# Value gradients of a recurrent attention's backward loop: from the memory keys alone to all 40 keys of a step

## The chip, the cores and the metric

One core of one Trainium2 chip runs the whole program. Its engines work side by side, each through its own list of instructions in a fixed order, and wait for one another by semaphores: TensorE (PE, with its weight loads PEld), VectorE (DVE), ScalarE (ACT), GpSimd (POOL) and the queue engine SyncE (SP), which only issues transfers. POOL issues transfers too, and each of those takes a place in its list. The metric is the device time of one launch in microseconds (us), the median of several runs.

## What is computed

The reference is the forward and the backward pass of one block: a layer norm, a recurrent attention A with a memory of 8 rows, a gated MLP B, and `out = x + A * silu(B)`. Outputs are `out` and the gradients of nine inputs, in bf16. The part that matters here is A's recurrence, cut from the reference:

```python
for s in range(n_seg):                     # S = 2048 rows, segments of 32: 64 steps
    xs = x[:, s * 32:(s + 1) * 32, :]
    h = concatenate([mem, xs], axis=1)     # 8 memory rows and 32 x rows
    q, k, v = (einsum('btd,dhe->bhte', h, W) for W in (Wq, Wk, Wv))   # 32 heads of 128
    p = softmax(where(mask, q @ k.T * scale, -1e9))
    o = einsum('bhqk,bhke->bhqe', p, v)
    o = einsum('bhte,hed->btd', o, Wo)
    mem = o[:, :8, :]                      # goes into the next step
    outs.append(o[:, 8:, :])
```

D is 640, so a weight is 640 x 4096. In the backward pass the steps run from the last to the first. The gradient of `v` of one step is, head by head, `p.T @ g`, where `g` is the gradient of the attention's output before `Wo`, over all 40 queries of the step. For the row gradient, `gv @ Wv.T` is added to `gk @ Wk.T` and `gq @ Wq.T`. The mask lets x queries see memory keys and earlier x keys, and memory queries see all 40 keys.

## The kernel before

The program runs in stages: layer norm and the forward pass of B; the forward recurrence of A (`recurrence`); the backward recurrence (`phase4_Abwd`, some 1810 to 2898 us of the profile); the weight stage (`phase6_Awgrads`, 2898 to about 4113 us), which forms the weight gradients of Wv, Wk and Wq and the row gradients of the x rows; the gradient of Wo; and the backward pass of B. In each stage `in_order` pins every engine to the written order.

**The backward loop.** `chain(t, gap)` is one step, t from 63 to 0. It holds a dependent chain: what it computes for the 8 memory rows is the gradient that the step before needs. Between its links it calls `gap("W0")`, `gap("W1")`, `gap("G1")` to `gap("G6")`, and `gap_of` fills each gap with work on the x rows, which depends on nothing in the chain. That work is cut into units: one tile of three steps (120 rows) and four heads (`tl, qd`). A unit goes through `ld` (transfers), `turn` (transposes of v and g rows), `dprob` (gradient of p), `dsoft` (gradient of the scores), `gmem` (what the x queries give to the memory keys, and to the memory values). Two or three units ride in each of 59 steps; the first ones are done ahead of the loop, and the last four steps have none.

The chain of a step, in the order of PE:

- `packed_half` twice (L306): the 32 rows in `gox` (8 memory rows, 24 x rows of a later step that ride along) times WoT, four column groups of 32 packed in the array; the result is copied to `sg` by DVE and by ACT, and stored to GOS by SP.
- `packed_sel` twice (L314): picks the 8 memory rows per group and turns them; DVE copies them to `gmT` (L1213).
- Two transposes of `gmT` (L1220), copied to `gOst`; 32 products of `gmT` with the turned values `vT` (`dprob_m`, L1226).
- `gkv(1, gOst, bdP)` (L1195, L1197): the value gradients of the 8 memory keys. `bdP` is the block diagonal of the memory queries' p, made by POOL at the step's start (L1182); `xp` adds what the x queries gave in `gmem`, loaded from GXP.
- `packed_out(gvT, WvT)` (L325): 64 matmuls, 8 weight columns each and 320 columns moving, into bank `pm`; 20 of them, then the transposes of the softmax gradient (L1236), then 44. DVE meanwhile forms `dS`.
- `gkv(0, ...)`, `packed_out(gkT, WkT)`, the q gradients (L1262), `packed_out(gqT, WqT)`: the same for k and q, all summed in `pm`.
- `fold_add` (L334, L336): ACT and DVE add the bank's two halves to `fs`. `fold_turn` (L352) turns it, DVE copies it to the next `gox` (L1283), and PE begins the next step. `fold_store` (L343) has POOL store the 8 memory rows, as two transfers.

`WARM = dict(G4=1)` puts one 128x512 product without use (L1430) between `fold_add` and `fold_turn`. The buffers that hold one step's loads are `vTb`, `Pm` and `Qsts` (two each of the last two), two `krbs` and one `xpb`. SP issues the loads in the written order: `loads` (L1151 to L1156), `load_k` (L1162 to L1169), `load_xp` (L1174), and `ld` for the units (L1307, L265, L1311). `ps.tile(..., tag="x", bufs=5)` are the five PSUM buffers that the units share.

**The weight stage.** Eight rounds of four heads (`qd`), 22 units each. `Fetch.ld` loads five units ahead: rows of DSR, PR and of g, q and k, with the memory rows fetched by POOL (`load_m`, L245). `s1` transposes dS, `s2` forms the row gradients of v, k and q from p or dS and the rows (i = 0, 1, 2), `s3` transposes these three for the x rows into `ring` (L1630), and `s4` multiplies them with WvT, WkT and WqT of the four heads, twelve matmuls per 128 rows and half of D, added into `acc` over the rounds (L1648, L1654). `wg` then forms the weight gradients of the round (L1667, three times 100 matmuls).

Of the kernel before, what the change touches and what calls it, by code (L numbers as in the profile page):

```python
# [16 lines left out]
P = 128  # L17
# [23 lines left out]
class K:  # L41
# [109 lines left out]
    def setup_dram(self):  # L151
# [15 lines left out]
        self.GXA = mk("GXA", (S, D))  # L167
        self.HRO = mk("HRO", (self.NR, D))
# [22 lines left out]
        self.GXP = mk("GXP", (self.NTL, P, 8, 3, 2, 32), F32)  # L191
# [6 lines left out]
        self.PM = mk("PM", (T, P, 80))  # L198
# [57 lines left out]
    def g_src(self, tl, c0, c1):  # L256
        nx = self.geo(tl)[2]
        x0 = 96 * tl
        if x0 >= self.GB0:
            return [(0, nx, self.GX0[x0 - self.GB0:x0 - self.GB0 + nx, c0:c1])]  # L260
        return [(0, 96, self.blk_src("g", 2 + tl, 0, 96, c0, c1))]

# [67 lines left out]
def fold_add(k, pm, pool, tag="fup"):  # L330

    fs = pool.tile([64, 320], BF16, name="fsum", tag="fsum")
    up = pool.tile([64, 320], F32, name="fup", tag=tag)
    k.nc.scalar.copy(up[:], pm[64:128, 0:320])  # L334
    for c in (0, 160):
        k.nc.vector.tensor_tensor(fs[:, c:c + 160], pm[0:64, c:c + 160], up[:, c:c + 160], ALU.add)  # L336
    return fs


def fold_store(eng, dst, fs):  # L340

    for b in range(2):
        eng.dma_start(dst[:, 320 * b:320 * b + 320], fs[32 * b:32 * b + 8, :])  # L343
# [211 lines left out]
def recurrence(k, W0, W4, Wv, Wk_, Wq, Wo, own, ps, banks):  # L555
    nc, tc = k.nc, k.tc
    D, DC, S, H, HD, T = k.D, k.DC, k.S, k.H, k.HD, k.T
    with tc.tile_pool(name="achain", bufs=1) as ch, \
# [39 lines left out]
        def chain(t, gap):  # L598
# [71 lines left out]
            nc.gpsimd.dma_start(k.PM[t].rearrange("p (a c) -> p a c", a=2), Pm[:])  # L670
# [24 lines left out]
            fs = fold_add(k, pm, ch)  # L695
# [387 lines left out]
def phase4_Abwd(k, out2, W0, W4, WT, own, ps, banks):  # L1083
# [20 lines left out]
    with tc.tile_pool(name="gst", bufs=1) as st, tc.tile_pool(name="gchain", bufs=1) as ch, \  # L1104
# [10 lines left out]
        Qsts = [two(k0[:, c:c + 256]) for c in (3072, 3328)]  # L1115
# [3 lines left out]
        bds = [PTs[1][:, 2 * i:2 * i + 2, :].rearrange("p a (h c) -> p a h c", c=8) for i in range(2)]  # L1119
        krbs = [st.tile([120, 2048], BF16, name="krb")[:], vt[0:120]]  # L1120
        bdm = st.tile([P, 16, 8], BF16, name="bdm")
        b16 = st.tile([P, 16], F32, name="b16")
        xpb = st.tile([P, 8, 2, 32], F32, name="xp")
# [6 lines left out]
        WARM = dict(G4=1)  # L1130
# [16 lines left out]
        def loads(t):  # L1147
# [4 lines left out]
            Pm = ch.tile([P, 2, 40], BF16, name="gPm", tag="gPm", bufs=2)  # L1152
            nc.sync.dma_start(Pm[:], k.PM[t].rearrange("p (a c) -> p a c", a=2))
            Qst = Qsts[t % 2]
            for a in range(2):
                nc.sync.dma_start(Qst[:, a, :], k.QM[t, :, a * 2048:(a + 1) * 2048])  # L1156
            ins[t] = vT, Pm, Qst

        def load_k(t):
            kr = krbs[t % 2][0:104]  # L1160
# [17 lines left out]
        def bd(eng, dst, src):  # L1178
            for a in range(2):
                v = src[:, a, 0:8]  # L1180
                v = bass.AP(tensor=v.tensor, offset=v.offset, ap=[list(v.ap[0]), [0, 16], list(v.ap[1])])
                eng.tensor_tensor(dst[:, a], bdm[:], v, ALU.mult)  # L1182

        def chain(t, gap):
# [3 lines left out]
            vT, Pm, Qst = ins.pop(t)  # L1188
            xp = xps.pop(t)
            bdP, bdS = bds  # L1190
            bd(nc.gpsimd, bdP, Pm)
            def gkv(i, lh, rh):
                pk = bB[:, 256 * i:256 * i + 256].rearrange("p (a c) -> p a c", a=2)
                for a in range(2):
                    nc.tensor.matmul(pk[:, a, :], lh[:, a, :], rh[:, a].rearrange("p h m -> p (h m)"), start=True, stop=True)  # L1195
                g_ = ch.tile([P, H, 8], BF16, name="gkv", tag=f"gkv{i}")
                nc.vector.scalar_tensor_tensor(g_[:].rearrange("p (u h) m -> p u (h m)", h=4),  # L1197
                                               pk.rearrange("p a (u c) -> p (a u) c", c=32), k.scale if i == 0 else 1.0,
                                               xp[:, :, i, :], op0=ALU.mult, op1=ALU.add)
                return g_  # L1200

            sg = ch.tile([P, 1024], BF16, name="gstg", tag="gstg", bufs=1)
# [6 lines left out]
            gap("W0")  # L1209
            packed_sel(k, pg, sg, 1)  # L1210
            gmT = ch.tile([P, 2, 8, 16], BF16, name="gmT", tag="gmT")
# [3 lines left out]
            nc.sync.dma_start(k.GOS[t // 4, :, :, t % 4].rearrange("g r c -> (g r) c"), sg[:])  # L1215
            gap("W1")
            gOst = ch.tile([P, 2, P], BF16, name="gOst", tag="gOst")
            pgo = bview(bB, P, 2, P, bf=True)
            for a in range(2):
                nc.tensor.transpose(pgo[:, a, :], gmT[:, a].rearrange("p q h -> p (q h)"), k.ident[:])  # L1220
            nc.vector.tensor_copy(gOst[:], pgo[:])
# [6 lines left out]
            gvT = gkv(1, gOst, bdP)  # L1228
            dprob_m(1)
            dPT = ch.tile([40, 2, P], BF16, name="dPT", tag="dPT")  # L1230
            nc.scalar.copy(dPT[:], psd.rearrange("p a q h -> p a (q h)"))
            gap("G1")
            packed_out(k, pm, gvT, WvT, True, False, 0, 5)
# [3 lines left out]
            pr = ch.tile([P, 2, 40], F32, name="gpr", tag="gpr")  # L1237
            nc.vector.tensor_tensor(pr[:], ps2[:], Pm[:], ALU.mult)
            Dm = ch.tile([P, 2], F32, name="Dm", tag="Dm")
            nc.vector.tensor_reduce(Dm[:], pr[:], axis=AX.X, op=ALU.add)  # L1240
            u = ch.tile([P, 2, 40], F32, name="gu", tag="gpr")
            nc.vector.tensor_tensor(u[:], ps2[:], bc_last(Dm[:], 40), ALU.subtract)
            dS = ch.tile([P, 2, 40], BF16, name="dSm", tag="dSm", bufs=2)
            nc.vector.tensor_tensor(dS[:], u[:], Pm[:], ALU.mult)
# [3 lines left out]
            packed_out(k, pm, gvT, WvT, False, False, 5, 16)  # L1248
            gkT = gkv(0, Qst, bdS)
# [3 lines left out]
            dST = ch.tile([104, 8, 16], BF16, name="dSTm", tag="dPT")  # L1253
# [10 lines left out]
            gqT = ch.tile([P, H, 8], BF16, name="gqT", tag="gqT")  # L1264
# [13 lines left out]
            fs = fold_add(k, pm, ch, "gstg")  # L1278
# [5 lines left out]
            fold_store(nc.gpsimd, k.m_rows(k.GWO, t - 1) if t > 0 else out2f, fs)  # L1284
            gap("G6")

# [71 lines left out]
        def gmem(tl, qd):  # L1358
# [4 lines left out]
            pk = ps.tile([P, 2, 4, nm], F32, name="gkp", tag="x", bufs=5)  # L1363
# [187 lines left out]
def phase6_Awgrads(k, X, W0, fetch, out0, out3, out4, out5):  # L1551
# [13 lines left out]
    with tc.tile_pool(name="h6i", bufs=3) as io, tc.tile_pool(name="h6", bufs=1) as hp, \  # L1565
# [136 lines left out]
        for _ in head(0):  # L1702
            pass
# [588 lines left out]
```

## Time and profile before

| | us |
|---|---|
| median of 3 runs (4697.81 to 4703.79) | 4698.75 |
| the profiled execution | 4684.61 |
| its span | 4682.7 |
| PE busy in the weight stage's matmuls L1648 | 459.9 |
| PE busy in its transposes L1630, gr rows | 134.5 |
| PE busy in the weight gradients L1667 | 521.7 |
| PE waiting for `fold_add` before L352 in the loop (62 times) | 24.0 |

How to read it: PE's busy time is the union of its matmuls, whose ends are modelled. So a group's busy time divided by its count gives what one costs in the stream, while "mean ns" is the length of one with its pipeline. In the lists in order of time, the first column is the start, the second the length of the whole group (x40 means forty instructions), and a bracket holds the idle time before it and what ended it. In the stage tables each pair of brackets holds an instruction count; the last three columns are the TensorE clock granted (1.00 is full speed), the mean busy share of the 16 DMA engines, and GB/s. A wait is put down to the engine whose semaphore came last.

### The profile page before, as it was taken

Reading aid. Unit: us, or ns where it says so; the run is one execution under the profiler, and the core shown is the slowest. Engines: PE = TensorE matmul, PEld = TensorE weight load, DVE = VectorE, ACT = ScalarE, POOL = GpSimd, SP = SyncE. Lnnn points to the kernel's source line nnn. Section 1 sums busy time; section 2 is a strip of 40 time slices with the busy share of each in tenths; the row PEclk is TensorE's granted clock in tenths of the full one; section 3 lists DMA queues with packets and bytes.
Section 4 is the critical chain, followed back from the end, with each engine's and each line's share of the span. In section 5 each row is a group of like instructions: output and inputs, shape, how many; then the busy total and the mean of one; then the engine's idle time right before and its main releaser. Section 6 shows DMA issues by size and latency. Waiting matters only on the chain. (4 is left out here: it accounts for less than half of the span.)

```text
span 4682.7 us, 159785 instructions
## 1 busy us (share of the span) xinstructions
PE 4466.5 (95%) x64504; PEld 2821.1 (60%) x64504; DVE 2244.7 (48%) x7156; ACT 1587.4 (34%) x4360; POOL 2098.4 (45%) x3528
## 2 busy tenths in 40 slices
PE   8999999999999898999999998999999999999999
PEld 4544555555555555666666665676667666666675
DVE  8734666666666534555555553343224432311460
ACT  5432555555544433333333332232223322200000
POOL 6532555555555423455444444354335533311440
PEclk9999999999999998999999999999999999999999
DMA  8773566666655677777777775664345543579783
GB/s 269 236 252 119 175 178 178 179 179 179 180 168 167 167 181 230 211 225 207 215 211 209 208 209 154 144 163 132 110 116 158 147 129 107 170 223 207 159 181 100
DMA packets 976843, 834.77 MB, mean 178 GB/s; under 512 B 518890, under 2 KB 858286, under 8 KB 974144
## 3 DMA queue, kind: packets, MB, share of 16 engines
q1 hardware_dynamic: 763879, 547.92, 42.2%
q0 software_dynamic: 129952, 228.13, 16.4%
q10 hardware_dynamic: 82275, 48.52, 4.0%
q8 instruction: 509, 8.34, 0.8%
q14 instruction: 228, 1.87, 0.1%
HBM read 472.66 MB, written 310.33 MB: 167 GB/s over the span
## 5 line engine op out<-in xcount | busy, mean ns | idle before, releaser
L1667 PE MATMUL wg<-gr,hr 128*128 128x512 bf16 x2400 | 521.7, 379 | 0.0
L1648 PE MATMUL g<-land,ghacc 128*128 128x320 bf16 x3072 | 459.9, 300 | 0.8
L1667 PEld LDWEIGHTS <-hr 128*128 128x128 bf16 x2400 | 233.9, 98 | 278.9
L306 PEld LDWEIGHTS <-hx 128*32 128x32 bf16 x10240 | 246.8, 96 | 229.1 <-issue 14.6
L1648 PEld LDWEIGHTS <-ghacc 128*128 128x128 bf16 x3072 | 289.2, 98 | 104.2 <-ACT ghacc L92 2.2
L90 DVE CAST wgo<-wg 128x512 bf16<-128x512 f32 x72 | 49.8, 692 | 471.2 <-PE wg L1667 471.2
L90 DVE CAST stg<-bank 128x512 bf16<-128x512 f32 x256 | 177.1, 692 | 158.6 <-PE bank L306 154.5
L880 POOL DMA_DIRECT2D OR<-xv x163 | 89.8, 551 | 361.1 <-ACT xv L92 338.5
L1613 POOL DMA_DIRECT2D GSP<-grs x48 | 25.5, 542 | 473.1 <-ACT grs L1605 472.0
L92 ACT COPY ghacc<-t6g 128x768 bf16<-128x768 bf16 (+1 forms) x176 | 137.1, 779 | 293.8 <-PE t6g L1630 284.5
L1324 POOL DMA_DIRECT2D VTD<-gvT x176 | 129.4, 742 | 218.7 <-ACT gvT L1323 209.5
L325 PEld LDWEIGHTS <-gkv 128*8 128x8 bf16 x8192 | 177.6, 86 | 82.2 <-issue 4.1
L832 POOL TENSOR_TENSOR xP<-xP,xrz 120x480 bf16<-120x480 bf16 x163 | 161.1, 988 | 76.0 <-DVE xrz L831 46.6
L812 ACT ACTIVATE xP<-xsp,xnm 120x120 bf16<-120x120 f32 (+1 forms) x540 | 186.1, 372 | 26.0 <-DVE xnm L794 25.9
L1654 DVE TENSOR_TENSOR ghacc<-ghacc,g 128x320 f32<-128x320 f32 x192 | 93.6, 487 | 209.9 <-PE g L1648 209.9
L336 DVE TENSOR_TENSOR fsum<-bank,fup 64x160 bf16<-64x160 f32 x254 | 69.5, 311 | 258.5 <-ACT fup L334 255.2
L92 ACT CAST wgo<-wg 128x512 bf16<-128x512 f32 x48 | 28.1, 585 | 479.8 <-PE wg L1667 407.0
L1371 POOL DMA_DIRECT2D GXP<-gks x157 | 91.0, 580 | 189.5 <-ACT gks L1369 188.8
L325 PE MATMUL bank<-Wo,oTm 128*32 128x320 bf16 x4032 | 154.2, 307 | 18.4 <-DVE oTm L684 18.4
L325 PE MATMUL bank<-WkT,gkv 128*8 128x320 bf16 x4096 | 162.8, 299 | 4.2 <-issue 2.2
L325 PE MATMUL bank<-WvT,gkv 128*8 128x320 bf16 x4096 | 166.4, 305 | 0.5 <-DVE gkv L1197 0.5
L306 PE MATMUL bank<-Wq,hx 128*32 128x512 bf16 x2560 | 161.6, 381 | 0.0
(389 smaller groups left out, 10916.1 us busy)
## 6 DMA issues: line engine op xcount, KB each, us to landing
QVS<-stg SPq DMA_DIRECT2D x128, 256.0 KB
kT<-VTD SPq DMA_DIRECT2D x64, 320.0 KB
PR<-xP POOLq DMA_DIRECT2D x168, 120.0 KB, 3.1
VTD<-gvT POOLq DMA_DIRECT2D x168, 120.0 KB, 4.0
land<-DSR SPq DMA_DIRECT2D x168, 120.0 KB
land<-PR SPq DMA_DIRECT2D x168, 120.0 KB
OR<-xv POOLq DMA_DIRECT2D x163, 120.0 KB, 3.0
orr<-OR SPq DMA_DIRECT2D x14, 1280.0 KB
```

What stands on the lines that cost most here:

```text
L90: return nc.vector.tensor_copy(out, in_)
L92: return nc.scalar.copy(out, in_)
L306: k.nc.tensor.matmul(bank[32 * g:32 * g + 32, :], x[:, dc, :], W[:, dc, c0:c0 + 512], start=(dc == 0), stop=(dc == k.DC - 1), tile_positio ...
L325: k.nc.tensor.matmul(pm[p0:p0 + nq, 0:320], x[:, h, :], W[:, h, 320 * b:320 * b + 320], start=(first and i == 0), stop=(last and i == 15), ...
L812: nc.scalar.activation(Pb[0:n, j, 0:n], sp[0:n, j, :], ACT.Exp, bias=nmx[0:n, j:j + 1], scale=k.scale, accum_out=Z[0:n, j:j + 1])
L832: eng.tensor_tensor(Pb[0:n, :, 0:n], Pb[0:n, :, 0:n], bc_last(rz[0:n], n), ALU.mult)
L880: q.dma_start(k.OR[120 * tl:120 * tl + n, c0:c0 + 512], v[0:n])
L1324: nc.gpsimd.dma_start(k.VTD[tl][:, :, h0:h0 + 4, :], vTq[:])
L1371: (nc.sync if (tl, qd) in pro else nc.gpsimd).dma_start(k.GXP[tl, :, qd, 0:ns], ks[:].rearrange("p s i h m -> p s i (h m)"))
L1648: nc.tensor.matmul(pg[:], ring[:, i, j, r0:r0 + P], Ws[qd][i][:, j, 320 * h:320 * h + 320], start=(i == 0 and j == 0), stop=(i == 2 and j ...
L1654: nc.vector.tensor_tensor(a, a, pg[:], ALU.add)
L1667: nc.tensor.matmul(pw[:], hr[:, tl, dc * P:(dc + 1) * P], grs[i][:, tl, :], start=(tl == 0), stop=(tl == NF - 1))
```

## The change

The value gradients of all 40 keys of a step are now formed in the chain. `vgrad` multiplies, per head, the 32 x rows of g (`xr`, loaded by SP) with their p (`prx`), and the 8 memory rows (`sg`) with theirs (`prm`): heads are split over four groups of 32 partitions, so 32 matmuls of 32 rows and 32 of 8 rows per step, 40 columns each, summed in four PSUM banks. ACT and DVE copy them to `gv`. `packed_out` takes the first 32 keys (8 of memory, 24 of x) in place of 8. The last 8 x keys of four steps are gathered in `lv` by POOL, and `extra` puts them through a packed product of their own every fourth step. The x rows' part of `gv @ Wv.T` is stored in a new tensor GXV, and the weight stage adds it once, in round 0, instead of forming it: `s3` and `s4` run over k and q alone. `gmem` and GXP lose their value half. To make room in SBUF, buffers are shared or single where they were two (`Pm`, `Qst`, `krb`, `fsum`, `seq`), and the useless product goes; the first unit's `turn` moves from W0 into the gap G4 of the step before, the second one's from W1 to G1. In the weight stage q's memory rows are loaded by SP, and the loads of `hr` are cut finer.

```diff
-def fold_add(k, pm, pool, tag="fup"):
+def fold_add(k, pm, up, fs):
...
-def fold_store(eng, dst, fs):
+def fold_store(eng, dst, fs, r0=0):
     for b in range(2):
-        eng.dma_start(dst[:, 320 * b:320 * b + 320], fs[32 * b:32 * b + 8, :])
+        eng.dma_start(dst[:, 320 * b:320 * b + 320], fs[32 * b + r0:32 * b + r0 + dst.shape[0], :])
...
-        WARM = dict(G4=1)
+        WARM = {}
...
+        def load_g(t):
+            tl, s = t // 3, t % 3
+            nc.sync.dma_start(xr, k.g_rows(t))
+            nc.sync.dma_start(prf, k.PR[tl][32 * s:32 * s + 32].rearrange("q (g h) c -> g q (h c)", g=4))
+            for g in range(4):
+                nc.sync.dma_start(prm[32 * g:32 * g + 8],
+                                  k.PM[t, g // 2].rearrange("(q b h) c -> b q h c", q=8, b=2)[g % 2])
+
+        def prx_copy(t):
+            tl, s = t // 3, t % 3
+            nx = k.geo(tl)[2]
+            nc.gpsimd.tensor_copy(prx[:, :, 8:40], prf[:, :, 32 * s:32 * s + 32])
+            nc.gpsimd.tensor_copy(prx[:, :, 0:8], prf[:, :, nx + 8 * s:nx + 8 * s + 8])
+
+        def vgrad(vb, lh, rh, n, j0, j1, first):
+            for j in range(j0, j1):
+                for g in range(4):
+                    p0 = 32 * g
+                    nc.tensor.matmul(vb[g][:, j, :], lh[p0:p0 + n, j * P:(j + 1) * P], rh[p0:p0 + n, j, :],
+                                     start=first and j == 0, stop=not first and j == 7, tile_position=(p0, 0), skip_group_check=True)
+
+        def extra(m, bank):
+            packed_out(k, bank, lv, WvT, True, True)
+            fs = fold_add(k, bank, up, ch.tile([64, 320], BF16, name="fsum", tag="fsum"))
+            for b in range(2):
+                nc.gpsimd.dma_start(k.GXV[128 * m:128 * m + 128, 320 * b:320 * b + 320].rearrange("(t r) d -> t r d", r=32)[:, 24:32],
+                                    fs[32 * b:32 * b + 32, :])
...
-            kr = krbs[t % 2][0:104]
+            kr = krbs[1][0:104]
...
-            bd(nc.gpsimd, bdP, Pm)
...
             packed_sel(k, pg, sg, 0)
             gap("W0")
+            vb = [bview(b_, P, 8, 40) for b_ in [bA] + [ps.tile([P, 512], F32, name="gvx", tag="x", bufs=5) for _ in range(3)]]
+            vgrad(vb, xr, prx, 32, 0, 8, True)
+            vgrad(vb, sg, prm, 8, 0, 4, False)
             packed_sel(k, pg, sg, 1)
...
+            vgrad(vb, sg, prm, 8, 4, 8, False)
...
+            if t > 0:
+                load_g(t - 1)
+            for g, e in ((0, 's'), (2, 'v'), (1, 's'), (3, 'v')):
+                k.copy(gv[:, 8 * g:8 * g + 8, :], vb[g], eng=e)
+            nc.gpsimd.tensor_copy(lv[:, :, 8 * (t % 4):8 * (t % 4) + 8], gv[:, :, 32:40])
             gap("W1")
-            gOst = ch.tile([P, 2, P], BF16, name="gOst", tag="gOst")
-            pgo = bview(bB, P, 2, P, bf=True)
-            for a in range(2):
-                nc.tensor.transpose(pgo[:, a, :], gmT[:, a].rearrange("p q h -> p (q h)"), k.ident[:])
-            nc.vector.tensor_copy(gOst[:], pgo[:])
...
             dprob_m(0)
-            gvT = gkv(1, gOst, bdP)
             dprob_m(1)
...
-            packed_out(k, pm, gvT, WvT, True, False, 0, 5)
+            packed_out(k, pm, gv32, WvT, True, False, 0, 5)
...
             fold_store(nc.gpsimd, k.m_rows(k.GWO, t - 1) if t > 0 else out2f, fs)
+            fold_store(nc.gpsimd, k.GXV[32 * t:32 * t + 24, :], fs, 8)
+            if t > 0:
+                prx_copy(t - 1)
             gap("G6")
...
                 nc.tensor.matmul(pk[:, 0, j, :], qv[0:n, 0, j * P:(j + 1) * P], dS[0:n, j, nx:n], start=True, stop=True)
-                nc.tensor.matmul(pk[:, 1, j, :], gor[0:n, j * P:(j + 1) * P], Pr[0:n, j, nx:n], start=True, stop=True)
...
                 if g == "W0":
                     ride_ld(t - 1)
-                    at(turn, t, 0)
-                elif g == "W1":
+                elif g == "G1":
                     at(turn, t, 1)
                     at(gmem_ld, t + 1, 2)
-                elif g == "G1":
                     at(dprob, t, 0)
...
+                    if t % 4 == 0:
+                        extra(t // 4, ps.tile([P, 512], F32, name="exb", tag="x", bufs=5))
                 elif g == "G4":
                     at(dprob, t, 2)
+                    at(turn, t - 1, 0)
...
         def s4(u, w, r0, h):
...
-            for i in range(3):
+            for i in range(2):
                 for j in range(4):
...
             if qd == 0:
-                nc.vector.tensor_copy(a, pg[:])
+                nc.vector.tensor_tensor(a, gvs[w][:, 320 * h:320 * h + 320], pg[:], ALU.add)
```

## The prediction

> **What bounds the kernel now.** I read the busy table, then the work and clock by stage, then the loop's PE and POOL in order of time. The profiled execution took 4684.61 us, 4682.7 of them its span; the median of the runs is 4698.75, so 14.1 us are added at the end.
>
> ```profile
> PE 4466.5 (95%) x64504; PEld 2821.1 (60%) x64504; DVE 2244.7 (48%) x7156; ACT 1587.4 (34%) x4360; POOL 2098.4 (45%) x3528
> ```
> ```profile
> 2350.00:2900.00 550.00, 522.34 (x12250) 340.61 (x12247) 279.18 (x1400) 171.98 (x574) 255.58 (x465) 0.99 0.67 194
> 2900.00:3000.00 100.00, 89.12 (x984) 70.61 (x984) 44.50 (x101) 39.40 (x65) 68.60 (x124) 0.91 0.87 209
> 3000.00:3500.00 500.00, 497.37 (x4148) 316.03 (x4147) 160.56 (x344) 133.29 (x222) 211.41 (x380) 1.00 0.47 127
> ```
>
> The columns are length, busy time of PE, PEld, DVE, ACT and POOL, the granted clock, the DMA share, GB/s. PE has no idle time to give in the weight stage (from 2898 on, eight rounds) and little in the backward loop (1810 to 2898). A matmul taken away there is time taken away; one added in the loop is time added, and so is any new wait of PE. Only the first round, 2900 to 3000, is at the transfers' limit (share 0.87).
>
> The loop's step is 17.0 us (the WoT product starts at 2511.32 and 2528.33). Its seam:
>
> ```profile
> 2510.15 0.78 PE L352 MATMUL bank<-sel,fsum 64*128 64x8 bf16 x6 [0.29 <-DVE fsum L336]
> ...
> 2511.32 2.34 PE L306 MATMUL bank<-WoT,hx 128*32 128x512 bf16 x40
> ...
> 2517.04 0.85 PE L325 MATMUL bank<-WvT,gkv 128*8 128x320 bf16 x20
> ```
> ```profile
> 2511.97 0.54 POOL L1371 DMA_DIRECT2D GXP<-gks  x1 [3.42 <-ACT gks L1369]
> 2512.50 1.05 POOL L343 DMA_DIRECT2D GWO<-fsum  x2
> ```
>
> The reader is to see that POOL is still issuing stores 2 us after PE began the next step. Nobody waits for them today.
>
> [...] In the last four steps, which have no filling work, the stretch between the WoT and the WvT product holds under 1 us of idle time among short matmuls; twice the clock fell:
>
> ```profile
> 2868.00:2869.50 1.50, 1.27 (x26) 0.97 (x27) 0.73 (x4) 0.00 (x0) 0.00 (x0) 1.00 0.45 175
> 2869.50:2871.00 1.50, 1.50 (x36) 0.82 (x32) 0.36 (x1) 0.36 (x1) 0.00 (x0) 0.72 0.07 14
> 2871.00:2872.50 1.50, 1.50 (x26) 0.79 (x26) 0.91 (x4) 0.00 (x0) 0.00 (x0) 0.50 0.77 223
> ```
>
> [...] The trace has two strips: 32 of L1262 (40 rows, 8 columns) in 0.52 us, 16 ns each; four strips it doesn't show. [...] the POOL lines above keep the written order too. [...] here GWO stores of 5 KB land 3.0 us after issue.
>
> **The change part by part.** Call F the start of fold_turn (2510.15), S the start of the WoT product, F + 1.17.
>
> *Weight stage, removed.* Of each s4's 12 matmuls 4 go: twelve take 1.63 us (2929.28 to 2930.91), so 0.543 each, x256 = 139 us. Of each s3's 12 transposes 4 go: 0.17 us (2930.91 to 2931.08), x176 = 30. Together 169, 21 per round. The seven later rounds: 148. There a unit takes PE 3.8 us on average now (84 us for 22), then 2.8; its loads (two of 120 KB, three of 96 and 72 KB of memory rows, 600 KB) then mean 214 GB/s, where the trace reached 236 at share 0.93 (3080 to 3095). SP issues a sixth load per unit (q's memory rows, moved from POOL); unhindered it issued five in 2.3 us (3090.28 to 3092.59), so six in 2.8, just the unit's time. POOL falls from 4.4 to 2.9 issues of 0.57. I put 2 us of stall on each round, 14. First round: at its limit before, and GXV's 2.6 MB come while WVT's 0.66 go; between 0 and -21, I take -6, with the hr load split finer. Sum -140 (-115 to -170). The qd 0 copy into ghacc becomes an add, 0.49 us each on DVE beside PE.
>
> *Loop, cheap parts.* GXP halves: 4 of 8 gkp matmuls per unit go, 0.11 us. The two gmT transposes (0.35 us with their wait), the value gkv product (0.22) and POOL's two mask products go. WARM's matmul goes from the wait for fold_add (E to F, 0.95 us), and the next step's first turn (0.42) comes into the same wait from W0, so both are free. ACT and DVE get two 128x320 copies each, 0.42 and 0.46 us between the rows for 128x256 and 128x384, and finish beside dprob. The packed WvT product costs 32-row weights no more than 8-row ones: Wo with 32 takes 2.35 us per 64 as well. SP goes from some 22 to 28 issues, at 0.46 about 13 us of a step: the single buffers (Qst, Pm, krb) make it wait, but each load still has over 8 us.
>
> *Loop, 64 small matmuls per step.* Between 8 ns (half of 16, four strips for two) and 26 (8 unpacked gkp take 0.21 us); I take 10: 0.64 us (0.5 to 1.7).
>
> *Loop, the new wait.* In the built order PE's first small matmul after packed_sel(0) waits for prx, which POOL copies at the end of its queue of the step before: GXP, two GWO stores, two GXV stores, then the two copies. GXP starts at F + 1.82; with 4 matmuls and one activation less F + 1.6, done F + 2.15; four stores at 0.525, F + 4.25; copies of 256 and 64 elements by the rows 128x120 (309 ns) and 128x768 (818 ns) 0.42 and 0.27, F + 4.94, seen by PE at F + 5.05. PE is there at S + 2.43 = F + 3.6. It waits 1.45 us (1.0 to 2.0). Behind that instruction stands all of the step. From its start T: x rows 0.32, mem rows 0.16, packed_sel(1), gmT 0.79 after that one's start (2325.93 to 2326.72 now), dprob's 32 at 33 ns from T + 1.4 to T + 2.46 (nothing fills W1 any more, 0.6 idle), then turn 0.42, gkp 0.11, gdp 0.29: the WvT product starts at T + 3.28 = S + 7.16 in place of S + 5.72. +1.44, less gkp's 0.11 in G3: 1.33 x 59 filled steps = 78. In the four steps without filling POOL has no GXP to issue and is in time: 0.
>
> *Loop, extra, every fourth step, 16 times.* A packed product of 64: 2.35 us. Its fsum shares the one buffer with the step's own: fold_add waits for both stores. They are issued 1.3 and 1.85 us after extra's end and land 3.0 later, 4.85; the step's adds are due at 2.35 + 0.57 = 2.92. Stall 1.95. 16 x 4.3 = 69 us (45 if the landing is hidden).
>
> *Loop's start:* prx's first load, 3 us.
>
> *Clock.* Between S + 2.4 and S + 7.2 PE now has 2.05 us idle and short matmuls else, a stretch of 4.8 us, longer and emptier than the one in which two of four fell. Each fall costs 0.45 + 1.08 = 1.5 us (WvT's 20 and 44 matmuls take 1.30 and 2.75 us from 2869.92 on, in place of 0.85 and 1.67). From 0 to 59 falls; since the turn and gdp remain at its end, I take one step in three: 20 x 1.5 = 30 us.
>
> Sum: 78 + 69 + 3 + 30 - 140 = +40. From 4684.6 that is 4725, on the scale of the median **4739**, taken as 4740.
>
> **The rivals.** (a) POOL is in time. PE waits for prx well under the 1.45 us and the clock holds: 40 - 59 x 1.45 - 30 = -76, 4623. For it: POOL is busy 45% only. Against it: the stores before the copies are in order, and no later work hides them. It decides as soon as the clock holds and the wait is under 1.25 us: then 40 - 30 - 12 is below zero. (b) The clock falls in nearly every step: 59 x 1.5 = 89, +99, 4798. [...] against it: gaps of 1.46 us in the loop (2266.8 to 2268.2) passed at full clock. (c) The rounds become bound by transfers or by SP's 2.8 us per unit, and give only 80: +100, 4799. For it: the first round's 0.87; against it: five units are loaded ahead and the product of 65 us per round lets the loads catch up. That the change misses its end is ruled out by the built counts: 2048 matmuls in s4 for 3072.
>
> **How the numbers follow.** Main case 0.42 (its own range 4705 to 4775), (a) 0.33, (b) 0.15, (c) 0.10. About 0.2% is what a measurement can tell from no change. (a) lies below by that much in nearly all of its span, the main case hardly ever: faster 0.32, same 0.08, slower 0.60. The range, with half of (a) and most of (b) and (c): 4620 to 4800.
>
> **What would show it.** In the changed profile: PE idle before the first prx matmul, released by POOL, 1.0 to 2.0 us in nearly every filled step; fold_add's add waiting on a DMA 16 times; granted clock below 1.00 in the loop; the loop some 150 to 180 us longer; s4's group at 307 us; the later rounds at some 130 us for 150. I am wrong if POOL's copies end before packed_sel(0), or if the weight stage loses under 110 us.

## The result

The changed kernel is slower: 4943.82 us in the median of four runs (4922.52 to 4950.91) against 4700.82, a ratio of 1.0509 with an interval of 1.0476 to 1.0543. The forecast was 4740 in a range that ended at 4800; the sign was right, the size was not. The profiled execution took 4946.79 us, its span is 4944.8, and 262.1 us longer than that of before.

The page of the changed kernel, its busy times and the clock granted in 40 slices of the span:

```profile
PE 4464.1 (90%) x66872; PEld 2806.8 (57%) x66872; DVE 2257.3 (46%) x7188; ACT 1576.9 (32%) x4328; POOL 2075.0 (42%) x3512
...
PEclk9999999999999988888888888889999999999999
```

PE is as busy as before (4466.5 us then), and the clock is down through the whole loop. The stage tables, loop and weight stage, first of the kernel before, then of the changed one (columns as before):

```profile
1804.00:2898.00 1094.00, 1041.11 (x24308) 679.59 (x24307) 562.06 (x2843) 350.63 (x1171) 516.73 (x940) 0.99 0.71 202
2898.00:4113.00 1215.00, 1198.39 (x10400) 783.97 (x10400) 411.82 (x889) 346.65 (x576) 541.61 (x973) 0.99 0.51 139
```

```profile
1814.00:3258.00 1444.00, 1185.33 (x28482) 787.24 (x28483) 579.27 (x2879) 394.16 (x1158) 610.65 (x1162) 0.86 0.60 170
3258.00:4375.00 1117.00, 1049.76 (x8671) 662.31 (x8672) 408.03 (x887) 294.05 (x576) 411.70 (x734) 0.98 0.53 147
```

The loop is granted 0.86 of the clock for 0.99 and moves 170 GB/s for 202, with PE idle for 259 us in it (53 before). So it is neither PE's work alone nor the total of bytes that fills it. In the weight stage PE's busy time fell by 149 us, but its idle time rose by 51 (17 before). The difference of the spans, by the starts of the WoT products and the stage borders of both traces:

| stretch | before, us | after, us | difference | forecast |
|---|---|---|---|---|
| up to the loop's first WoT product | 1804.1 | 1814.8 | +10.7 | +3 (start) |
| first step | 21.8 | 30.8 | +9.0 | |
| the 62 steps up to the last WoT product | 1055.9 | 1388.6 | +332.7 | +177 |
| last step's rest | 16.1 | 23.9 | +7.8 | |
| weight stage | 1215 | 1117 | -98 | -140 |
| Wo's gradient, B's backward pass | 570 | 570 | 0 | 0 |

A filled step without `extra` takes 21.2 us on average where it took 17.1, one with `extra` 26.9 where it took 16.9. The seam of two steps, PE in order of time:

```profile
2303.01 2.34 PE L313 MATMUL bank<-WoT,hx 128*32 128x512 bf16 x40 [0.19 <-DVE hx L1335]
2305.35 0.27 PE L321 MATMUL bank<-sel,gs 128*128 128x32 bf16 x4
2306.70 0.17 PE L1199 MATMUL bank<-prx,gor 32*128 32x40 bf16 x1 [1.09 <-POOL prx L1193]
...
2320.17 0.37 PE L1374 MATMUL gvpt<-ident,kT 120*128 120x120 bf16 x4 [0.79 <-DMA kT<-QVS]
...
2326.72 1.00 PE L1278 MATMUL bank<-gmT,kT 128*40 128x8 bf16 x32 [0.37 <-DMA DSR<-kT]
2330.92 0.56 PE L1374 MATMUL gvpt<-ident,kT 120*128 120x120 bf16 x4 [3.20 <-DMA kT<-QVS]
...
2332.35 1.52 PE L332 MATMUL bank<-WvT,gv 128*32 128x320 bf16 x20
...
2333.98 2.04 PE L332 MATMUL bank<-WvT,gv 128*32 128x320 bf16 x44
```

The first bracket is the wait that the forecast named. The other two on L1374 it did not name: the `turn` of a unit finds its v rows not yet loaded, which did not happen before (0.3 us in the same thousand microseconds). And the WvT product at the end of the list runs at a lower clock: 1.52 and 2.04 us where 0.85 and 1.67 stood. (The wait for `prx` alone does not always do this: the product of the step before, after the gap of 1.09 us, took 0.86 and 1.68.) The waits of PE between 1830 and 2830 us (total, times, longest):

```profile
PE bank L1199 <- POOL prx L1193: 70.5, 30, 11.8
PE gvpt L1374 <- DMA kT<-QVS: 29.7, 16, 3.3
PE bank L357 <- DVE fsum L341: 29.3, 23, 3.9
```

Why the units' loads are late is seen on SP, in order of time after the step's WoT product:

```profile
2307.95 0.59 SPq L1183 DMA_DIRECT2D gor<-GOS  x1
2308.63 0.58 SPq L1184 DMA_DIRECT2D gor<-PR  x1
2309.31 1.77 SPq L1186 DMA_DIRECT2D prm<-PM  x4
2311.17 1.64 SPq L1361 DMA_DIRECT2D kT<-QVM  x1
2312.86 0.59 SPq L272 DMA_DIRECT2D kT<-QVS  x1
2315.61 0.32 SPq L272 DMA_DIRECT2D kT<-GOS  x1
2318.43 0.32 SPq L1365 DMA_DIRECT2D kT<-PR  x1
```

SP pauses twice for over 2 us between single issues. In the trace its transfers carry eight semaphores in turn, and of 1764 issues between 1830 and 3240 us none began before the last update of the transfer eight places ahead of it. The GOS load of 2315.61 stands eight places after `gor<-GOS`, the PR load of 2318.43 after `gor<-PR`; of the 126 issues eight places after a load into `gor` 124 began within 0.1 us of its last update. SP's own list of waits in the same thousand microseconds names them:

```profile
SPq L1365 <- DMA gor<-PR: 73.5, 28, 3.2
SPq L1174 <- DMA gor<-PR: 43.4, 16, 4.6
SPq L272 <- DMA gor<-GOS: 36.5, 16, 2.9
```

So the two new loads of `load_g` (256 KB each) took 7.7 and 9.8 us: the semaphores' records have their last updates 7.65 and 9.78 us after the issues, and the two late issues of SP come 0.02 us after these. In the meantime the DMA engines were not full:

```profile
2308.00:2309.00 1.00, 1.00 (x33) 0.96 (x33) 0.74 (x2) 0.48 (x2) 0.12 (x1) 1.00 0.87 306
...
2311.00:2312.00 1.00, 1.00 (x36) 0.78 (x32) 0.90 (x4) 0.00 (x0) 0.54 (x1) 1.00 0.44 96
2312.00:2313.00 1.00, 1.00 (x27) 0.56 (x16) 0.66 (x4) 0.08 (x1) 0.00 (x0) 1.00 0.39 127
2313.00:2314.00 1.00, 1.00 (x31) 0.76 (x27) 1.00 (x10) 0.73 (x4) 0.00 (x0) 1.00 0.37 134
```

In the 7 us with both loads pending the mean share of the 16 engines is 0.53, and for three of them it is 0.37 to 0.44. In the semaphores' records each of the two has five updates, one about 1.0 us after the issue and four late ones (5.9 to 7.65 us after it for the GOS load above, 8.3 to 9.8 for the PR load). From 1830 to 3240 us the last one comes 7.45 us after the issue for `gor<-GOS`, 6.09 for `gor<-GX` (g of other steps) and 9.35 for `gor<-PR`, in the median of 42, 21 and 63. The larger load `kT<-VTD` (320 KB) has sixteen updates, the last after 3.99 us in the median of 63; a load of 128 rows (`d_rows128`) or of 32 rows (`b_split`) has sixteen too. The two slow loads have the four head groups as slowest dimension of their source. That this shape is what slows them was my estimate, which `d_rows128` and `b_split` try; which engines a transfer ran on the traces do not show.

### The profile page after: what moved, and what is told of

Its sections match the earlier page's. It is cut to its first block, busy times and chain, and to the rows that moved or that the text cites. A ratio compares the mean times of both kernels' runs of the same rounds, so it can differ in the third digit from the quotient of the medians.

```text
span 4944.8 us, 165433 instructions
## 1 busy us (share of the span) xinstructions
PE 4464.1 (90%) x66872; PEld 2806.8 (57%) x66872; DVE 2257.3 (46%) x7188; ACT 1576.9 (32%) x4328; POOL 2075.0 (42%) x3512
## 3 DMA queue, kind: packets, MB, share of 16 engines
q14 instruction: 236, 1.93, 0.1%
## 4 chain that ended last, share of the span: by engine, by line
PE 40%; DMA 12%; issue 5%; POOL 4%; DVE 3%; SPq 1%; ACT 1%; ACTq 0%; POOLq 0%; DVEq 0%
PE wg L1736 10%; PE bank L332 6%; PE g L1715 4%; DMA land<-DSR 4%; PE oa L1884 4%; PE wa L2272 2%; PE bank L313 2%; PE r6p L1658 1%; PE pgxb L2205 1%; DMA GXV<-fsum 1%; PE bank L1278 1%; PE t6g L1691 1%; DMA kT<-QVS 1%; DMA kT<-GOS 1%; PE t L1648 1%
## 5 line engine op out<-in xcount | busy, mean ns | idle before, releaser
L1715 PE MATMUL g<-land,ghacc 128*128 128x320 bf16 x2048 | 326.7, 305 | 0.0
L332 PE MATMUL bank<-WvT,gv 128*32 128x320 bf16 x4096 | 233.6, 390 | 0.0
L1715 PEld LDWEIGHTS <-ghacc 128*128 128x128 bf16 x2048 | 193.1, 99 | 65.8
L1673 POOL DMA_DIRECT2D GSP<-grs x48 | 25.5, 542 | 466.0 <-ACT grs L1665 466.0
L313 PE MATMUL bank<-WoT,hx 128*32 128x512 bf16 x2560 | 183.0, 441 | 11.8 <-DVE hx L1335 11.1
L246 POOL DMA_DIRECT2D land<-KS x256 | 144.9, 571 | 65.9 <-PE r6p L1658 51.0
L92 ACT COPY ghacc<-t6g 128x384 bf16<-128x384 bf16 (+1 forms) x176 | 82.6, 469 | 275.5 <-PE t6g L1691 272.7
L332 PE MATMUL bank<-WkT,kT 128*8 128x320 bf16 x4096 | 161.5, 299 | 2.8 <-DVE kT L1245 1.7
L313 PE MATMUL bank<-Wv,hx 128*32 128x512 bf16 x2560 | 161.6, 381 | 0.0
L332 PEld LDWEIGHTS <-gv 128*32 128x32 bf16 x4096 | 120.8, 120 | 63.7
```

Source lines behind the costliest of these rows:

```text
L92: return nc.scalar.copy(out, in_)
L246: eng.dma_start(d, src if src.shape[0] > 1 else src[0])
L313: k.nc.tensor.matmul(bank[32 * g:32 * g + 32, :], x[:, dc, :], W[:, dc, c0:c0 + 512], start=(dc == 0), stop=(dc == k.DC - 1), tile_positio ...
L332: k.nc.tensor.matmul(pm[p0:p0 + nq, 0:320], x[:, h, :], W[:, h, 320 * b:320 * b + 320], start=(first and i == 0), stop=(last and i == 15), ...
L1715: nc.tensor.matmul(pg[:], ring[:, i, j, r0:r0 + P], Ws[qd][i][:, j, 320 * h:320 * h + 320], start=(i == 0 and j == 0), stop=(i == 1 and j ...
```

## The experiments

Each ratio is to the kernel before on the same chip. "Plain" and "extra" are mean steps of the loop (44 and 15 of them), "low clock" counts, of 63, the WvT products (with the transposes between them) during which the clock record is below full speed. Such a product takes 3.9 us in the median in the changed kernel, for 2.60 before.

| kernel | median, us | ratio (interval) | plain | extra | low clock |
|---|---|---|---|---|---|
| before | 4700.82 | 1 | 17.1 | 16.9 | 2 |
| changed | 4943.82 | 1.0509 (1.0476 to 1.0543) | 21.2 | 26.9 | 54 |
| d_rows128 | 4853.35 | 1.0325 (1.0288 to 1.0363) | 19.9 | 24.8 | 43 |
| a_noload | 4860.91 | 1.0339 (1.0316 to 1.0362) | 19.7 | 24.5 | 45 |
| b_split | 4911.26 | 1.0441 (1.0425 to 1.0457) | 20.8 | 25.5 | 54 |
| c_pool | 4891.73 | 1.0399 (1.0377 to 1.0421) | 20.4 | 24.7 | 46 |
| e_prx | 4954.67 | 1.0515 (1.0489 to 1.0540) | 20.7 | 27.6 | 46 |
| i_rows_prx | 4785.12 | 1.0154 (1.0125 to 1.0183) | 18.4 | 24.1 | 25 |
| g_split_prx_fs | 4867.86 | 1.0328 (1.0299 to 1.0357) | 20.6 | 23.4 | 47 |
| m_rows_prx_fs | 4750.02 | 1.0088 (1.0067 to 1.0109) | 18.6 | 22.1 | 31 |
| k_pool_prx_fs | 4823.80 | 1.0256 (1.0229 to 1.0284) | 19.6 | 23.0 | 31 |
| p_warm | 4733.94 | 1.0086 (1.0070 to 1.0101) | 18.7 | 21.1 | 17 |
| h_wq | 4982.62 | 1.0572 (1.0544 to 1.0600) | | | |
| j_out_act | 4920.37 | 1.0450 (1.0427 to 1.0474) | | | |
| n_nb6 | 4900.38 | 1.0408 (1.0382 to 1.0434) | | | |
| q_all | 4762.62 | 1.0145 (1.0129 to 1.0160) | 19.3 | 23.4 | 14 |
| s_all_sp | 4789.40 | 1.0213 (1.0175 to 1.0250) | 20.3 | 23.0 | 34 |
| r_all_split | 4660.92 | 0.9924 (0.9900 to 0.9949) | 18.3 | 20.4 | 5 |

### The two loads

Same issues, same bytes, another source (so the value gradients are of other numbers), so that the slowest dimension is 128:

```diff
-            nc.sync.dma_start(xr, k.g_rows(t))
-            nc.sync.dma_start(prf, k.PR[tl][32 * s:32 * s + 32].rearrange("q (g h) c -> g q (h c)", g=4))
+            nc.sync.dma_start(xr, k.KS[t // 4, :, :, t % 4].rearrange("g r c -> (g r) c"))
+            nc.sync.dma_start(prf.rearrange("p h c -> p (h c)"), k.KS[t // 4, :, :, (t + 1) % 4].rearrange("g r c -> (g r) c"))
```

> The two 256 KB loads of load_g read other rows (a whole 128 x 1024 block of KS), so the value gradients of the output are of other numbers; number of issues, bytes, waits and places are those of the changed kernel, only the source's slowest dimension is 128 in place of 4. Theory 1 (k): a load whose slowest dimension is 4 [...] takes 8 to 10 us, and SP's issue eight places later waits for it. Then the step falls from 22 us to 18 to 19, the clock goes back above 0.93 in the loop, the time to 4660 to 4780. Theory 2 (SP issues too much, 28 issues for 22): 4920 to 4950, no change. Theory 3 (the bytes, 512 KB more per step): no change either.

It fell by 1.8% of the time before, and 94 us of the loop's 62 steps went. The bytes and SP's count of issues were the same, so of the three theories only the first is left for this part: the two loads land late (7.7 and 9.8 us in the seam above), and SP's later issues wait for them. It expected more, though: the time stayed above the 4780 of its range, the plain step at 19.9 us for 18 to 19, and the clock of the loop at 0.89 for over 0.93. In this kernel the turn's loads are in time, although `turn` stands in the changed kernel's place; so the earlier place alone did not make them late. What remains is the forecast's wait, and the wait of `extra`:

```profile
PE bank L1199 <- POOL prx L1193: 49.2, 32, 3.5
PE bank L357 <- DVE fsum L341: 34.1, 24, 4.1
```

Without the loads after the first step:

```diff
-            nc.sync.dma_start(xr, k.g_rows(t))
-            nc.sync.dma_start(prf, k.PR[tl][32 * s:32 * s + 32].rearrange("q (g h) c -> g q (h c)", g=4))
+            if t == T - 1:
+                nc.sync.dma_start(xr, k.g_rows(t))
+                nc.sync.dma_start(prf, k.PR[tl][32 * s:32 * s + 32].rearrange("q (g h) c -> g q (h c)", g=4))
```

> The two 256 KB loads are made for the first step only; all later steps use its rows, so the output is of other numbers. Theory 1 (k) expects the same as with full-width loads, or up to 40 us less, since SP issues 2 fewer: 4640 to 4760. Theory 2 (number of SP issues) expects 2 of 28 to give 1.2 us a step at most: 4860 to 4900. Theory 3 (bytes) expects this one fast and the full-width loads slow, near 4940.

The same as with full-width loads, within the intervals. So 512 KB per step cost nothing as bytes that these runs resolve. The time misses the first theory's range by 100 us and stands at the edge of the second's, but the full-width kernel is as fast with both issues in place, so it is not their number.

The right rows, one load per group of heads (32 rows slowest), or both loads left as they are and issued by POOL:

```diff
-            nc.sync.dma_start(xr, k.g_rows(t))
-            nc.sync.dma_start(prf, k.PR[tl][32 * s:32 * s + 32].rearrange("q (g h) c -> g q (h c)", g=4))
+            for g in range(4):
+                nc.sync.dma_start(xr[32 * g:32 * g + 32], k.g_rows(t)[g])
+                nc.sync.dma_start(prf[32 * g:32 * g + 32],
+                                  k.PR[tl][32 * s:32 * s + 32].rearrange("q (g h) c -> g q h c", g=4)[g])
```

> Each of the two loads becomes four of 32 rows (one strip each): the right rows, 64 KB each, slowest dimension 32[...]; but 34 issues of SP per step for 28. Theory 1 (k): faster than the changed kernel, 4700 to 4850, what is left over the full-width case being SP's six more issues of 0.6 us. Theory 2 (SP issues): slower than the changed kernel by up to 6 x 0.6 x 60 = 200 us, above 5000.

> The two loads are issued by POOL after the stores that stand there, SP has 26 issues and none of these two among its eight in flight. Theory 1 (k): the transfers still have a slowest dimension of 4, but SP no longer waits for them, so SP's later loads come in time: 4680 to 4850; the copies into prx wait for them on POOL if they take 10 us. Theory 2 (SP issues): 4860 to 4900. Theory 3 (bytes): no change, 4920 to 4950.

Both are faster than the changed kernel, and both miss the first theory's range; the second (4892) lies in the range of the theory of SP's issues. The split one gains in spite of six more issues of SP, which theory 2 said it could not; but it gets only 0.7% where full width got 1.8%. I take the rest to be those issues: in its trace SP issues 34.6 transfers per step in 17.4 us, more than a whole step before, where the changed kernel's 28.6 took 14.8. The last two kernels below support it: the same eight parts take 4789 us by SP and 4661 by POOL. Loads by POOL take SP out of it, and get 1.1%; as both theories expect a gain from that, this run does not tell them apart. One transfer of the right rows at full width was not tried, and in no run were the buffers that the change made single (`Pm`, `Qst`, `krb`) given back.

### POOL's order

```diff
+            if t > 0:
+                prx_copy(t - 1)
             packed_out(k, pm, gqT, WqT, False, True)
...
             fold_store(nc.gpsimd, k.GXV[32 * t:32 * t + 24, :], fs, 8)
-            if t > 0:
-                prx_copy(t - 1)
```

> The changed kernel with the two prx copies put ahead of the step's last fold on POOL, before the GXP, GWO and GXV stores instead of after them. Theory of the prediction (PE waits for POOL's order of work): the wait before the first prx matmul, 1 to 2.5 us in a filled step, goes, and with it part of the clock falls: 4944 down to 4790 to 4850. Rival (the slow loads alone set the pace, the wait on prx only shows it): the copies then wait for the loads' landing in the new place as well, and it stays within 40 us of 4944.

> The loads of full width (other rows of KS, so value gradients of other numbers) and the prx copies put ahead of the stores, together. If slow loads and POOL's order are two separate costs, their gains add: 4853 less another 100 to 150, so 4700 to 4750, the plain step near 17.7 us and the extra step near 22.5. If the one covers the other, it stays near the better of the two alone. If the clock falls come from the lack of filling work rather than from the wait, the WvT product still takes over 3.5 us and the gain is under 70.

On the changed kernel the edit alone gained nothing, as the rival said. The wait on `prx` was gone, but PE stood elsewhere for as long; the waits of `e_prx`:

```profile
PE gvpt L1374 <- DMA kT<-QVS: 71.1, 22, 6.1
...
PE bank L1199 <- POOL prx L1193: 1.4, 2, 0.8
```

PE reached the turn earlier and waited there for loads that SP issues at its own pace. While SP was the slower one here, the wait on POOL cost nothing of its own. With the full-width loads the same edit gave 1.7%, 72 us of the loop; the time missed its range of 4700 to 4750. Its last theory (clock falls from the lack of filling work) is not met either, since the gain is over 70; but 25 of the WvT products still ran at low clock. That kernel also shows plain steps with none of the three losses, seven of 44 at 16.9 to 17.1 us; one of them on PE:

```profile
2482.79 0.26 PE L321 MATMUL bank<-sel,gs 128*128 128x32 bf16 x4
2483.59 0.27 PE L321 MATMUL bank<-sel,gs 128*128 128x32 bf16 x4
2484.43 1.00 PE L1278 MATMUL bank<-gmT,kT 128*40 128x8 bf16 x32 [0.37 <-DVE gmT L1264]
...
2486.16 0.86 PE L332 MATMUL bank<-WvT,gv 128*32 128x320 bf16 x20
```

Between the two lines of L321 stand 48 of the 64 small matmuls, 0.5 us, and the WvT product runs at full clock (0.86). So the new arithmetic of a step fits into its old 17 us.

### The fold's buffer

```diff
-            fs = fold_add(k, bank, up, ch.tile([64, 320], BF16, name="fsum", tag="fsum"))
+            fs = fold_add(k, bank, up, lv[0:64].rearrange("p h c -> p (h c)")[:, 0:320])
```

> Loads of 32 rows (8 for 2), prx copies early, and the extra product's folded sum in storage of its own (in lv, free by then), so that the step's own fold need not wait for its stores. Expected by the prediction's steps: the stall of about 2 us at 16 steps goes (32 us) besides the prx wait (100 to 150): from 4911 to 4730 to 4780. If the step with extra is longer for another reason than the shared buffer, it stays 5 us above the others.

> All three cures in the loop: the two loads of full width (other rows of KS, so value gradients of other numbers), the prx copies early, and the extra product's folded sum in storage of its own. Theory (three separate costs, and the small matmuls are cheap): plain steps 17.0 to 17.5 at clock 0.97 or more, extra steps 19.5 to 20.5, the loop 1090 to 1130 us; total 4785 less 50 to 90, so 4695 to 4735. Rival (the thinned stretch itself drops the clock): plain steps stay spread between 17 and 20, total above 4750.

> The right rows again, the two loads of slowest dimension 4 issued by POOL, prx copies early, the extra sum in its own storage. Theory (SP's loads need only not to queue behind the slow ones): near the full-width kernel with the same cures, 4720 to 4790; the prx copies may wait for the loads' landing on POOL and hold its stores. Rival (26 issues of SP and 30 of POOL are too many in any case): above 4830.

All three stayed 15 to 90 us above their ranges. The stall itself was real: from `i_rows_prx` to `m_rows_prx_fs`, which differ in this buffer alone, the step with `extra` fell from 24.1 to 22.1 us and the ratio by 0.7%. In `g_split_prx_fs` the turn's loads are late for 81 us (34 issues of SP). In `m_rows_prx_fs` plain steps are still spread from 17 to 24 us, with 31 products at low clock: the clock's loss is there without any wait on `prx`. In the changed kernel 14 folds wait for a GXV store to land (16 steps have an `extra`), 61 us of DVE's time in all.

### The clock

```diff
-        WARM = {}
+        WARM = dict(W1=1)
...
-                    nc.tensor.matmul((bA if g in ("W1", "G2") else bB)[:], k.ident[:], WqT[:, 0, 0:512], start=True, stop=True)
+                    nc.tensor.matmul((bA if g == "G2" else bB)[:], k.ident[:], WqT[:, 0, 0:512], start=True, stop=True)
```

> The kernel with all three loop cures (loads of full width from other rows, so value gradients of other numbers), and one matmul of 512 columns whose result nobody reads between the last small matmul and dprob, where PE idles 0.37 us for gmT. Theory (the clock falls because the stretch between the WoT and the WvT product is thin): fewer falls, granted clock in the loop 0.94 up to 0.97 or more, 4750 less 15 to 40. Rival (falls come from the waits for late loads elsewhere): no change, or up to 20 us more for the matmul itself.

The low products fell from 31 to 17, which supports the theory, but the ratio stayed (1.0086 for 1.0088): in the profile the 62 steps took 1184.8 us for 1196.7, and a gain of that size is not resolved. The remaining time is not settled by it.

The clock records of the traces say more of when it falls. They change only at multiples of one interval of 3.41 us. The seam shown above, cut at three of these borders, in the changed kernel:

```profile
2324.53:2327.94 3.41, 1.93 (x100) 1.75 (x99) 1.28 (x4) 1.06 (x4) 2.29 (x6) 1.00 0.65 137
2327.94:2331.35 3.41, 0.43 (x5) 0.46 (x6) 0.00 (x0) 0.19 (x1) 0.06 (x1) 0.50 0.65 187
...
2334.77:2338.18 3.41, 3.41 (x104) 2.23 (x100) 2.67 (x17) 0.33 (x2) 0.00 (x0) 1.00 0.29 72
```

PE was busy for 1.93 us of the interval before the fall. In the 62 steps the clock fell 70 times, for one to four intervals; PE's busy share of the interval before was 0.46 in the median and at most 0.88. After 222 intervals it held, with a share of 1.00 in the median and at least 0.49. The two overlap, so the busy share alone does not decide it; what does was not measured. And the loss is not in the WvT product alone. Both products of the 62 steps, before and in the changed kernel (busy time after the bar):

```profile
L325 PE MATMUL bank<-WvT,gkv 128*8 128x320 bf16 x3968 | 157.8, 301 | 0.0
L306 PE MATMUL bank<-WoT,hx 128*32 128x512 bf16 x2480 | 145.2, 380 | 5.9 <-DVE hx L1283 1.2
```
```profile
L332 PE MATMUL bank<-WvT,gv 128*32 128x320 bf16 x3968 | 225.9, 389 | 0.0
L313 PE MATMUL bank<-WoT,hx 128*32 128x512 bf16 x2480 | 176.2, 439 | 11.5 <-DVE hx L1335 10.9 <-ACT xqT L1383 0.2
```

That is 68 and 31 us more for as many matmuls, and the transposes of `turn` add 18 (134.7 for 116.9): 117 us. With full-width loads it is 59, 25 and 12, 96 us.

### The weight stage

PE's waits there for a unit's first rows, in the changed kernel:

```profile
PE t L1648 <- DMA land<-DSR: 55.9, 51, 4.2
```

> The changed kernel with q's memory rows loaded by POOL again in the weight stage, the loop untouched. Theory (SP has six issues per unit, with eight in flight, and cannot feed a unit in 2.8 us): PE's 56 us of waits for land<-DSR fall below 20, rounds near 131 us for 137, total 4944 less 30 to 50. Rival (600 KB per unit at the transfers' rate): no change within 10 us.

```diff
-            if nm == "q":
...
-            else:
-                k.load_m(r, tl, nm, c0, c0 + 512, nc.gpsimd)
+            k.load_m(r, tl, nm, c0, c0 + 512, nc.gpsimd)
```

Slower by 0.6% in place of faster: the waits for DSR fell to 20 us, but 23 for QVS and 14 without a named cause came in their place, for loads of both engines. POOL fetches these rows in up to three pieces where SP needed one, so this run does not clear SP's count alone; it shows that moving the issue to POOL is no cure. What SP does in each weight product is one line of its list:

```profile
3493.73 58.21 SPq L1740 DMA_DIRECT2D out_dram<-wgo  x15
```

For 58 of 66 us it stands in front of stores that wait for the product, with the next round's loads behind them. Those stores by ACT, and then also six units ahead (`NB` 6 for 5) in the space that the value weights left:

```diff
-                nc.sync.dma_start(outf[2 - i][dc * P:(dc + 1) * P, c0:c0 + 512], ot[:])
+                nc.scalar.dma_start(outf[2 - i][dc * P:(dc + 1) * P, c0:c0 + 512], ot[:])
```

> The changed kernel with the weight products' output stores issued by ACT instead of SP; the loop untouched. In the changed kernel SP stands 58 of the 66 us of each weight product in those 15 stores, each waiting for its product, and the loads of the next round's units queue behind. Theory (loads kept out of the product's time): one or two more units are loaded in each product, PE's waits for land<-DSR fall from 56 to under 35 us, total 4944 less 15 to 35. Rival (the five buffers alone limit it): no change within 8 us.

> As the kernel with stores from ACT, and six units loaded ahead for five (the space that the value weights left). Theory (the unit segment is at the transfers' rate, share 0.7 to 0.99, and each unit loaded in the product's time is 2.8 us less in it): another 10 to 25 us less than with the stores alone, rounds 131 to 134 us for 137. Rival (limited by something other than how much is loaded ahead): as with the stores alone.

The waits for DSR, in the first and in the second:

```profile
PE t L1648 <- DMA land<-DSR: 31.9, 33, 2.8
```
```profile
PE t L1648 <- DMA land<-DSR: 16.3, 12, 3.0
```

A round went from 137.5 to 133.0 and 129.6 us (149.8 before the change). Both gave what was expected, the second with slightly shorter rounds.

### Everything together

> Everything on the right rows: loads by POOL, prx copies early, own storage for the extra sum, the filling matmul, output stores of the weight products by ACT, six units loaded ahead. If the measured gains add (4824, less 44 of the weight stage, less 15 to 40 of the clock): 4740 to 4770, still slower than before. Rival (they overlap, since a late POOL holds everything): 4790 or more.

> As the one with everything, but each POOL load split into four of 32 rows, slowest dimension 32[...], at 6 more POOL issues of 0.55 us per step. If what is left in the POOL version is the slow landing of the two loads: 20 to 40 us less, 4710 to 4740. If POOL has no room for 3.3 us more: slower by 30 to 100.

> As the one with everything, but the two loads issued by SP in four parts each, 34 issues of SP per step. With prx copies and own storage alone this form took 4868; less 44 and 15 to 40: 4785 to 4810, SP's issues still making turn loads late. A result under 4760 would mean that SP's count was not what was left.

The three hold the copies put early, the sum's own storage, the filling product, the stores by ACT and the six units, and differ only in the two loads: by POOL as they were, by POOL in four parts of 32 rows each, by SP in four parts each. `q_all` and `s_all_sp` came out as expected; `r_all_split` went below its range. It is 102 us faster than `q_all`, with six more issues per step on the same engine, and beats the kernel before by 0.8% (0.5 to 1.0). Not all of this is the change's own: the last two edits are worth 44 us in the changed kernel, more than the 37 by which it wins, and the stores by ACT would have fitted the kernel before as well. That was not run; PE's waits for DSR are only 4 us there. POOL's issues show the time to landing, the last column, first in `q_all`, then in `r_all_split`:

```profile
gor<-PR POOLq DMA_DIRECT2D x64, 256.0 KB, 8.4
```
```profile
gor<-PR POOLq DMA_DIRECT2D x256, 64.0 KB, 4.2
```

The loop of `r_all_split`:

```profile
1840.00:3010.00 1170.00, 1079.23 (x27952) 724.41 (x27948) 576.65 (x2849) 386.25 (x1144) 843.33 (x1633) 0.98 0.75 203
```

The clock is back at 0.98 and the transfers at 203 GB/s (1.00 and 205 before the change, from 1840 to 2880 us). Of the 102 us, 91 lie in the 62 steps, where PE's idle time falls from 145 to 89 us; why it was more than expected was not taken apart further.

## Why the prediction was right in sign and wrong in size

The sum was +40, and the span grew by 262. By the forecast's own terms:

- *"SP goes from some 22 to 28 issues ... each load still has over 8 us."* This step failed. It counted issues and bytes, and did not ask how long each new load holds one of SP's eight places. The two loads took 7.7 and 9.8 us, and SP's eighth issue after each waited, so that the loads of `turn` came late. Shown by `d_rows128`: 94 us of the 62 steps, a term that the sum did not have. The count itself was right (22.6 and 28.6 issues).
- *The new wait*, 1.45 us in nearly every filled step, 86 us: right in place and near in sum. PE's idle time before the first prx matmul is 96 us in the 62 steps (78 with full-width loads), but 17 of the 59 filled steps have none. That it is a cost of its own was right only once the loads were cured (`e_prx` against `i_rows_prx`).
- *Extra*, 4.3 us more than a plain step: 5.6 measured, 4.9 with full-width loads, of which some 2 go with the buffer (1.95 forecast; its terms, 4.85 less 2.92, give 1.93).
- *Clock*, one step in three, 20 x 1.5 = 30 us: mis-sized. 54 of 63 products ran low, 52 more than before, and the WoT product and `turn`, which the term left out, ran low too: 117 us in place of 30, and 96 with full-width loads (43 products). Rival (b), a fall in nearly every step, was nearer.
- *Small matmuls*, 0.64 us a step: right, about 0.6.
- *Loop's start*, 3 us: 20 with the first step, and the last step 8 more.
- *Weight stage*, -140: -98, under the 110 that the prediction named as a sign of being wrong. The work went nearly as forecast: s4's group 326.7 us (459.9 before; 307 forecast), s3's 83.5 (134.5). The failed term is the stall of 14: "the product of 65 us per round lets the loads catch up". SP cannot load then, since it stands in the stores; PE waited 56 us for DSR. Rival (c) named the place, but with the transfers or the issues as cause; `j_out_act` and `n_nb6`, with the same issues and bytes, show that when the loads may start was a cause; PE's wait falls to 16 us, and a round to the 130 us that was forecast.

Added to the +40: 94 for the loads, 42 for the weight stage, 24 for start and end give 200. The other 62 are what the loop with full-width loads has over the forecast's 177 (238 against it); the clock, 96 in place of 30, is 66 and `extra` some 5 to 10. That is a little more than 62; the terms overlap, and the small rest was not taken apart.

Rival (a) needed POOL in time and the clock held. In the changed kernel neither was so; `r_all_split` has both, and lands at 4661 (4623 forecast), on its side of the line, but with the help of the 44 us of the weight stage.

## What to carry to other kernels

Of each transfer that a change adds, look at how long it takes to land, and at which issue waits for it on its queue. Here two loads were cheap as bytes (4853 us with full-width loads, 4861 with none) and still took 7.7 and 9.8 us and held up what stood eight places behind them; so a new load's shape is worth a run of its own. Where an engine issues stores that wait for a result, as SP did for 58 of 66 us, ask what loads stand behind them. And try suspected costs together as well as alone: moving the copies gained nothing until the loads were cured, and 1.7% after.

## What was not expected of the hardware

Two loads of 256 KB with a slowest dimension of 4 took 7.7 and 9.8 us while the DMA share was 0.53 in the mean. Issued by POOL, the PR load landed in 8.4 us in the median (`q_all`); cut into parts of 32 rows, each landed in 4.2 us (`r_all_split`), and eight such issues on POOL beat two by 102 us. The clock was low in the WvT product of 54 of 63 steps. In the interval of 3.41 us before a fall in the changed kernel's 62 steps PE's longest gap was 1.45 us in the median of the 70 falls, and 0.35 us in the one where it was shortest: the clock also fell where PE was never idle for long.
